# The eighth block pair of a 2048 x 2048 product by Strassen, with its weights prepared earlier and on VectorE

## The chip, the cores and the metric

One core of one Trainium2 chip runs the kernel. The metric is the device time of one execution in microseconds (us), the median of three runs. The core has TensorE (PE, matrix products into PSUM), VectorE (DVE), ScalarE (ACT), GpSimd (POOL) and SyncE (SP, which here only issues transfers). Each engine works through its own list of instructions in order, and waits on semaphores for the others.

## What is computed

```python
S, D, H, Dh = 2048, 512, 32, 16
Fh = 688
x = A_x                                    # (1, 2048, 512) bf16
# A: linear attention
q, k, v = split_heads(x @ wqkv)
phi(t) = concat(softmax(t @ w_phi), softmax(-(t @ w_phi)))
o = (phi(q) @ (phi(k)^T v)) / (phi(q) @ sum_s phi(k) + 1e-6)
a = o @ wo
# B: spatial gating
z  = gelu(x @ w_in)                        # (2048, 1376)
z1 = z[:, :Fh];  z2 = layernorm(z[:, Fh:])
g  = w_sp @ z2 + b_sp[:, None]             # (2048 x 2048) @ (2048 x 688)
b  = (z1 * g) @ w_out
# mix
s = sigmoid((x * gate_w).sum(-1))
out = s * a + (1 - s) * b
```

## The kernel before

The tokens are cut into 16 tiles of 128. The work comes in four stretches.

**z2 half (up to 24 us).** For each token tile, `z2_tile` multiplies x by the second half of w_in (eight matmuls of 344 columns into a PSUM tile `zp`, of which there are three), ScalarE takes the gelu into `z2raw`, and VectorE takes mean and variance (two L226, one L227). After every fourth tile `z2_norm` lets GpSimd compute `rstd` (L287, L290) and VectorE write the normalised `z2all` (four L292). x arrives transposed by SP's transfers (L142, L149).

**z1 half (24 to 44 us).** `z1_tile` does the same product with the first half of w_in, and ScalarE's gelu (L280) writes `z1all`; a `zp` tile comes free when its gelu has read it. Two calls of `fold` multiply the query and key weights with w_phi (after tiles 6 and 11) and ScalarE copies the results out (L336, L334). `z_sum` lets VectorE form the sums T1 to T4 of z2 (eight L400).

**Main stretch (44 to 125 us).** Sixteen steps, one for each key tile. A step holds the product of the next key tile (`k_tile`, L438), of the value tile (`v_tile`, L481), the accumulation of an earlier tile (`kv_acc`, L498), one entry of the list `steps` of the spatial product, and in the steps of `Q_AT` a query tile (`q_tile`). For each key or query tile ScalarE takes two exponentials (L442), VectorE a sum over 1024 elements (L446) and a reciprocal, and GpSimd a scaling (L461, L462). For a value tile VectorE writes `vr` (L487), which frees the bank `V_BANK` that all value tiles but the second share.

**Last stretch (from 125 us).** The rest of `steps`, the attention outputs and the final products of each token tile.

**The spatial product.** w_sp has 16 row tiles. Row tiles p and p+8 are a pair. `w_load(p)` brings a pair in by two transposing transfers (L170, ring of four buffers `wsp`). For the pairs 1 to 7 (`MIXED`) the 2 x 2 block product of the pair with z2 is done by Strassen's method in Winograd's form: seven products P1 to P7 of eight matmuls each (`product`, L563) instead of eight. Pair 0 (`PLAIN`) is done directly by `plain`: four pieces (two row tiles, two column halves) of sixteen matmuls each (L531), one piece in each of the steps 0 to 3.

A Strassen pair needs its weights prepared. `w_size` (ScalarE, L341, twice) sums absolute values of the two row tiles, a small activation adds the two sums into `wsum16` (L346), `w_level` multiplies that with ones on TensorE (L350), so that every partition has the level, and VectorE takes `wdown` and `wup` from it (L352, L355). `w_scale` (ScalarE, L374) scales the second row tile in place, and `w_sum` (VectorE, L361, L381, L383) forms S3, S1, S2 and S4, in that order. S4 overwrites A12, so it comes after P2. When a product is done, ScalarE or VectorE takes it from PSUM: `seed` after P1 or P4, `scaled` after P6, P7 and P4 (L545), an activation after P2 (L583), and `plus` after P7 and P3 (VectorE, L570); `gated` multiplies each result into `z1all` (GpSimd, L577). P5, and then P3, accumulate in one PSUM bank, and the `plus` of P7 reads that bank between them.

**What sets the order.** On TensorE and ScalarE the program's order is kept as written (`manual_schedule`); on the other engines a scheduler orders by readiness at build time. `steps` is a list that is filled pair by pair, and `work_at` says in which step a pair's `w_size`, `w_scale`, `w_sum` and `w_load` are called. SP issues all transfers of the first stretches in one queue: x, w_in, the bias row `brow`, the first part of the query and key weights, eight small `wphi` pieces, the second part, the value weights `wv_sb`, then three pairs of w_sp.

Of the kernel before, what the change touches and what calls it, by code (L numbers as in the profile page):

```python
# [14 lines left out]
P = 128  # L15
# [20 lines left out]
PLAIN = (0,)  # L36
MIXED = (1, 2, 3, 4, 5, 6, 7)
# [4 lines left out]
def kernel(  # L42
# [112 lines left out]
    nc.sync.dma_start(out=brow[0:NT, :], in_=B_b_sp.rearrange("(t p) -> t p", p=P))  # L155
    heads = A_w_phi.rearrange("(kc u) e f -> u e kc f", u=8)
    for qk in (1, 0):
        nc.sync.dma_start_transpose(
            out=wqkT[:, qk * NDT:(qk + 1) * NDT, :], in_=A_wqkv[:, qk * D:(qk + 1) * D])
        for u in range(8 if qk == 1 else 0):  # L160
            us = slice(u * DH, (u + 1) * DH)
            nc.sync.dma_start(out=wphi[us, :, us], in_=heads[u])
    nc.sync.dma_start(out=wv_sb[:, :, :], in_=A_wqkv[:, 2 * D:3 * D].rearrange("(dt p) n -> p dt n", p=P))
# [9 lines left out]
    for p in range(3):  # L173
        w_load(p)
# [54 lines left out]
    def z2_tile(tt):  # L229
        z2_out(tt, z_mm(tt, w_z2, FH + 1))  # L230
# [44 lines left out]
    def z1_of(tt, c0, c1):  # L275
        return z1all[:, tt, c0:c1]
# [62 lines left out]
    def w_size(p, h):  # L339
        mute = ring.tile([P, NT * P], BF16, name="mute", bufs=1)  # L340
        nc.scalar.activation(  # L341
            out=mute[:, :],
            in_=wraw[p][:, h * NT:(h + 1) * NT, :].rearrange("p s c -> p (s c)"),
            func=AF.Abs, accum_out=wsum[:, p, h:h + 1])
        if h == 1:
            nc.scalar.activation(  # L346
                out=wsum16[:, p:p + 1], in_=wsum[:, p, 1:2], func=AF.Identity, bias=wsum[:, p, 0:1])

# [8 lines left out]
    HALVED = (5, 6)  # L357

# [13 lines left out]
    def w_scale(p):  # L372
        tail = wraw[p][:, NT:2 * NT, :].rearrange("p s c -> p (s c)")
        nc.scalar.activation(out=tail.bitcast(FP16), in_=tail, func=AF.Copy, scale=wup[:, p:p + 1])  # L374
# [103 lines left out]
    def v_tile(tt, rk, bank):  # L478
        v_ps = bank_tile(bank)
# [13 lines left out]
        return vr  # L493
# [33 lines left out]
    def plain(t, j):  # L527
        x = bank_tile(next_turn("mm", 2))[:, 0:HF]
        h = t // HS
        for st in range(NT):  # L530
            nc.tensor.matmul(  # L531
                x, lhsT=wraw[t % HS][:, h * NT + st, :], rhs=z2all[:, st, j * HF:(j + 1) * HF],
                start=(st == 0), stop=(st == NT - 1))
        zu = z1_of(t, j * HF, (j + 1) * HF)
        nc.vector.scalar_tensor_tensor(
            out=zu, in0=x, scalar=bT[:, t:t + 1], in1=zu, op0=ALU.add, op1=ALU.mult)
# [175 lines left out]
    Q_AT = (1, 3, 6, 9, 12, 15)  # L712
    with tc.manual_schedule(engines={mybir.EngineType.PE, mybir.EngineType.Activation}):
# [3 lines left out]
        for tt in range(NT):  # L717
# [3 lines left out]
            late = steps[0][0][0] is product and steps[0][0][2] in (1, 6)  # L721
# [3 lines left out]
            pend.append((tt, ek, v_tile(tt, rk, V_BANK if tt != 1 else X_TAGS[2])))  # L725
# [112 lines left out]
```

## Time and profile before

| | |
|---|---|
| three runs | 199.76, 200.1, 200.7 us; median 200.1 |
| the profiled execution | 199.89 us, of which the span from first to last instruction is 198.2 |
| granted TensorE clock | 1.0 |
| z2 half, z1 half | TensorE to 24.06 us, to 44.12 us |
| ScalarE and VectorE, 46 to 62 us | 15.4 and 13.5 of 16 us busy |
| DMA engines, 22 to 26 us | 0.17 and 0.07 mean busy share in two slices of 2 us |

Times below are us from the start of the span, durations us or, where marked, ns. PE is TensorE's matmul row and PEld its weight load. A row of instructions gives line, engine, operation, tiles, shapes and count, then the busy total in us and the mean of one in ns, then the engine's idle time in front of them and what ended it.

### The profile page before, as it was taken

How to read it: one execution, taken by the hardware profiler on the slowest of the kernel's cores; microseconds unless marked ns; L12 is line 12 of the kernel's file. 1: busy time of each engine (PE TensorE's matmuls, PEld its weight loads, DVE VectorE, ACT ScalarE, POOL GpSimd, SP SyncE). 2: the span in 40 equal slices, each digit the busy share in tenths (PEclk: the TensorE clock that was granted, in tenths of full speed). 3: DMA queues.
4: the chain of work that ended last, by engine and by line, in shares of the span. 5: the costliest groups of instructions: out<-in, count | busy, mean ns of one | idle time of the engine just before them, and what ended most of it. 6: DMA issues, size and time to landing. Idle time of an engine off the chain costs nothing.

```text
span 198.2 us, 3988 instructions
## 1 busy us (share of the span) xinstructions
PE 193.4 (98%) x1466; PEld 115.6 (58%) x1484; DVE 144.4 (73%) x268; ACT 136.2 (69%) x216; POOL 88.2 (45%) x132
## 2 busy tenths in 40 slices
PE   8999999999999999999999999999999999999994
PEld 4666666665555665565565566665555555654542
DVE  4478977914989999798798796998968569554300
ACT  3466667889899679789789788569675476232222
POOL 6021023000552685885795788645536245420400
PEclk9999999999999999999999999999999999999999
DMA  6799479999803930750870666697688898595261
GB/s 193 134 190 218 86 156 194 207 202 208 244 3 64 200 58 0 159 109 0 160 107 3 132 133 69 143 205 146 138 161 181 113 220 149 119 149 132 65 147 53
DMA packets 89210, 26.50 MB, mean 134 GB/s; under 512 B 84536, under 2 KB 89064, under 8 KB 89192
## 3 DMA queue, kind: packets, MB, share of 16 engines
q1 hardware_dynamic: 86448, 23.32, 62.2%
q10 hardware_dynamic: 2600, 2.42, 5.0%
q0 software_dynamic: 144, 0.52, 0.8%
q8 instruction: 11, 0.18, 0.4%
q14 instruction: 7, 0.06, 0.1%
HBM read 3.45 MB, written 2.10 MB: 28 GB/s over the span
## 4 chain that ended last, share of the span: by engine, by line
PE 92%; SPq 2%; DMA 2%; DVE 1%; issue 1%; DVEq 0%
PE mm L563 27%; PE zp L208 19%; PE mm L438 14%; PE mm L634 8%; PE mm L481 7%; PE mm L629 6%; PE mm L531 5%; DMA oT<-o 2%; PE kvacc L498 2%; PE at L604 2%; SPq L524 1%; PE zp L239 1%; DVE o L615 1%; SPq L475 1%; PE zp L327 0%
## 5 line engine op out<-in xcount | busy, mean ns | idle before, releaser
L208 PE MATMUL zp<-w_z,xT 128*128 128x344 bf16 (+1 forms) x254 | 38.5, 311 | 0.0
L577 POOL TENSOR_TENSOR z1all<-c,z1all 128x344 bf16<-128x344 f32 x28 | 25.5, 916 | 21.0 <-DVE c L570 7.2
L563 PEld LDWEIGHTS <-wsp 128*128 128x128 f16 (+1 forms) x280 | 26.6, 98 | 13.9
L208 PEld LDWEIGHTS <-xT 128*128 128x128 bf16 x254 | 24.4, 98 | 12.3 <-DMA xT<-in_A_x_dram 0.4
L563 PE MATMUL mm<-z2all,wsp 128*128 128x344 f16 x168 | 27.9, 309 | 0.0
L341 ACT ACTIVATE mute<-wsp 128x2048 bf16<-128x2048 bf16 x14 | 26.8, 1914 | 0.4 <-ACT ob L646 0.4
L446 DVE TENSOR_REDUCE zs<-eq 128x64 f32<-128x1024 bf16 x16 | 19.3, 1209 | 7.5 <-ACT eq L442 7.5
L646 ACT ACTIVATE ob<-mm,g_inv 128x512 bf16<-128x512 f32 (+1 forms) x16 | 10.9, 680 | 19.8 <-PE mm L634 17.8
L446 DVE TENSOR_REDUCE zs<-ek 128x64 f32<-128x1024 bf16 x16 | 19.2, 1203 | 7.2 <-ACT ek L442 7.2
L634 PE MATMUL mm<-w_out_sb,uT 128*128 128x512 bf16 (+2 forms) x101 | 23.3, 366 | 0.1
L461 POOL TENSOR_TENSOR ratio<-zs,rk 128x32 f32<-128x32 f32 x16 | 8.2, 511 | 32.8 <-DVE rk L455 29.7
L442 ACT ACTIVATE eq<-mm 128x512 bf16<-128x512 f32 x32 | 17.3, 593 | 6.9 <-PE mm L438 6.4
L563 PE MATMUL mm<-zmix,wmix 128*128 128x344 f16 x112 | 18.6, 309 | 0.0
L563 PE MATMUL mm<-zmix,wsp 128*128 128x344 f16 x112 | 18.6, 309 | 0.0
L462 POOL TENSOR_TENSOR eq<-eq,ratio 128x512 bf16<-128x512 bf16 x16 | 17.4, 1089 | 1.3
L438 PEld LDWEIGHTS <-xT 128*128 128x128 bf16 x128 | 11.8, 98 | 10.5
L462 POOL TENSOR_TENSOR ek<-ek,ratio 128x512 bf16<-128x512 bf16 x16 | 17.9, 1119 | 0.0
L442 ACT ACTIVATE ek<-mm 128x512 bf16<-128x512 f32 x32 | 17.3, 603 | 0.5 <-PE mm L438 0.2
L374 ACT ACTIVATE wsp<-wsp,wup 128x2048 f16<-128x2048 bf16 x7 | 14.0, 2001 | 4.5 <-DVE wup L355 4.5
L223 ACT ACTIVATE z2raw<-zp 128x688 bf16<-128x688 f32 x16 | 11.9, 745 | 7.4 <-PE zp L208 7.0
L481 PE MATMUL mm<-wv_sb,xT 128*128 128x512 bf16 x62 | 16.3, 379 | 0.1
L629 PE MATMUL mm<-wo_t,oT 128*128 128x512 bf16 (+2 forms) x65 | 16.3, 366 | 0.2
(100 smaller groups left out, 308.2 us busy)
## 6 DMA issues: line engine op xcount, KB each, us to landing
out_dram<-ob ACTq DMA_DIRECT2D x14, 128.0 KB, 2.5
w_z<-in_B_w_in_dram SPq DMA_DIRECT2D x2, 344.0 KB, 5.8
w_out_sb<-in_B_w_out_dram SPq DMA_DIRECT2D x1, 640.0 KB, 4.8
wv_sb<-in_A_wqkv_dram SPq DMA_DIRECT2D x1, 512.0 KB
wo_t<-in_A_wo_dram POOLq DMA_DIRECT2D x1, 512.0 KB, 5.8
w_z<-in_B_w_in_dram ACTq DMA_DIRECT2D x2, 172.0 KB, 3.4
w_z<-in_B_w_in_dram SPq DMA_DIRECT2D x2, 172.0 KB, 3.3
wsp<-in_B_w_sp_dram SPq DMA_TRANSPOSE x16, 5.2
```

What stands on the lines that cost most here:

```text
L208: nc.tensor.matmul(zp[:, j, 0:n], lhsT=xT[:, dt, tt * P:(tt + 1) * P], rhs=wt[:, dt, j * HF:j * HF + n], start=(dt == 0), stop=(dt == NDT ...
L341: nc.scalar.activation(out=mute[:, :], in_=wraw[p][:, h * NT:(h + 1) * NT, :].rearrange("p s c -> p (s c)"), func=AF.Abs, accum_out=wsum[: ...
L374: nc.scalar.activation(out=tail.bitcast(FP16), in_=tail, func=AF.Copy, scale=wup[:, p:p + 1])
L438: nc.tensor.matmul(ps[:, :], lhsT=xT[:, dt, tt * P:(tt + 1) * P], rhs=w[:, dt, :], start=(dt == 0), stop=(dt == NDT - 1))
L442: nc.scalar.activation(out=e[:, :, a, :], in_=ps[:, :].rearrange("p (h f) -> p h f", f=DH), func=AF.Exp, scale=1.0 - 2.0 * a)
L446: nc.vector.tensor_reduce(out=z[:].rearrange("p h a -> p (h a)"), in_=e[:].rearrange("p h a f -> p (h a) f"), axis=AX.X, op=ALU.add,)
L462: nc.gpsimd.tensor_tensor(out=e[:, :, 1, :], in0=e[:, :, 1, :], in1=ratio[:, :, None].to_broadcast([P, H, DH]), op=ALU.mult)
L481: nc.tensor.matmul(v_ps[:, :], lhsT=xT[:, dt, tt * P:(tt + 1) * P], rhs=wv_sb[:, dt, :], start=(dt == 0), stop=(dt == NDT - 1))
L563: nc.tensor.matmul(x, lhsT=w_part(p, wa)[:, st, :], rhs=zsums[zb][:, st, :], start=(k in OPENS and st == 0), stop=(st == HS - 1), skip_gro ...
L577: nc.gpsimd.tensor_tensor(out=zu, in0=o, in1=zu, op=ALU.mult)
L629: nc.tensor.matmul(acc, lhsT=oTs[n][:, g, :], rhs=wo_t[:, g, c0:c1], start=start and g == 0, stop=stop and g == NG - 1)
L634: nc.tensor.matmul(acc, lhsT=uTs[n][:, ft, :], rhs=w_out_sb[:, ft, c0:c1], start=start and ft == 0, stop=stop and ft == NFT - 1)
```

## The change

Pair 0 goes from `plain` to the seven products. Its list entries are P1 and P5 in step 0, P2 in step 1, P6, the next pair's P1 and P7 in step 2, P4 and P3 in step 3. Pair 1 has its P1 already done in step 2, so step 4 holds two products instead of three. From step 5 on the entries are the same. Its preparation lies in the z1 half: VectorE takes the largest absolute value of the second row tile (`w_peak`) in place of one `w_size`, ScalarE keeps the `w_size` of the first row tile, VectorE adds twice the one to the other (`w_both`), `w_level(0)` stands on TensorE behind z1 tile 12, and VectorE scales the tail and forms S3, S1 and S2. One half of pair 1 is measured with `w_peak` too, and pair 1 is scaled on VectorE. `brow`, `wphi` and `wv_sb` are loaded from GpSimd's queue, ahead of its first `veps`, and no longer from SP's; SP loads four pairs of w_sp at the start. `z_sum` is called behind the tiles 1 to 8, the second `fold` behind tile 10. The second value tile goes to the upper half of `kvacc` and no longer to a bank of the products. Queries are in the steps 1, 4, 8, 11, 13 and 15, in place of 1, 3, 6, 9, 12 and 15.

In the built program VectorE's list for the z1 half reads: the first `zmix`, four `z2all`, three `zmix`, the first peak, four `zmix`, `wsum16` of pair 0, the peak of pair 1, `wdown`, `wup`, the scaling of pair 0, S3, S1, S2, and then the first two key sums of the main stretch. GpSimd's list has the ten transfers, then both `veps` and both `rstd` of the first eight tiles, and VectorE writes the first eight `z2all` together behind the first half statistics of tile 8.

```diff
-PLAIN = (0,)
-MIXED = (1, 2, 3, 4, 5, 6, 7)
+MIXED = tuple(range(NP))
...
+    def load_small():
+        heads = A_w_phi.rearrange("(kc u) e f -> u e kc f", u=8)
+        nc.gpsimd.dma_start(out=brow[0:NT, :], in_=B_b_sp.rearrange("(t p) -> t p", p=P))
+        for u in range(8):
             us = slice(u * DH, (u + 1) * DH)
-            nc.sync.dma_start(out=wphi[us, :, us], in_=heads[u])
-    nc.sync.dma_start(out=wv_sb[:, :, :], in_=A_wqkv[:, 2 * D:3 * D].rearrange("(dt p) n -> p dt n", p=P))
+            nc.gpsimd.dma_start(out=wphi[us, :, us], in_=heads[u])
+        nc.gpsimd.dma_start(
+            out=wv_sb[:, :, :], in_=A_wqkv[:, 2 * D:3 * D].rearrange("(dt p) n -> p dt n", p=P))
...
-    for p in range(3):
+    for p in range(4):
         w_load(p)
...
+    def w_peak(p, h):
+        nc.vector.tensor_reduce(
+            out=wsum[:, 0, 1:2], in_=wraw[p][:, h * NT:(h + 1) * NT, :].rearrange("p s c -> p (s c)"),
+            axis=AX.X, op=ALU.max, apply_absolute_value=True)
+
+    def w_both(p, h):
+        nc.vector.scalar_tensor_tensor(
+            out=wsum16[:, p:p + 1], in0=wsum[:, 0, 1:2], scalar=2.0, in1=wsum[:, p, 1 - h:2 - h],
+            op0=ALU.mult, op1=ALU.add)
...
+    SCALED_ON_DVE = (0, 1)
...
     def w_scale(p):
         tail = wraw[p][:, NT:2 * NT, :].rearrange("p s c -> p (s c)")
+        if p in SCALED_ON_DVE:
+            nc.vector.tensor_scalar(
+                out=tail.bitcast(FP16), in0=tail, scalar1=wup[:, p:p + 1], scalar2=None, op0=ALU.mult)
+            return
         nc.scalar.activation(out=tail.bitcast(FP16), in_=tail, func=AF.Copy, scale=wup[:, p:p + 1])
...
             z2_tile(tt)
+            if tt == 2:
+                load_small()
...
         b_T()
-        turn["zp"] += 1
         for tt in range(NT):
             z1_tile(tt)
-            if tt % 2 == 1:
-                z_sum(tt // 2 // 4, tt // 2 % 4)
-            if tt in (6, 11):
+            if 0 < tt < 9:
+                z_sum((tt - 1) // 4, (tt - 1) % 4)
+            if tt in (6, 10):
                 later = fold(1 if tt == 6 else 0)
-            if tt in (7, 8, 12, 13):
+            if tt in (7, 8, 11, 12):
                 later.pop(0)()
+            if tt == 5:
+                w_peak(0, 1)
+            if tt == 9:
+                w_size(0, 0)
+            if tt == 10:
+                w_both(0, 1)
+            if tt == 12:
+                w_level(0, zp_tile()[:, 0, :])
+                w_scale(0)
+                w_sum(0, 3)
+                w_sum(0, 1)
+            if tt == 14:
+                w_peak(1, 0)
...
-    LOAD_AT = {3: 1, 4: 4, 5: 7, 6: 10, 7: 13}
-    SIZE_AT = {1: (0, 1, 2), 2: (2, 3, 4), 6: (14, 16, 17), 7: (18, 19, 20)}
+    LOAD_AT = {4: 3, 5: 6, 6: 9, 7: 12}
+    SIZE_AT = {1: (0, 0, 2), 6: (14, 16, 17), 7: (18, 19, 20)}
...
+        if p == 0:
+            steps.append(first[:2])
+            del first[:2]
+            n = 1
         steps += [first, middle, [(product, p, 4), (product, p, 3)]]
...
-    Q_AT = (1, 3, 6, 9, 12, 15)
+    Q_AT = (1, 4, 8, 11, 13, 15)
...
+            if tt == SIZE_AT[1][2]:
+                w_both(1, 0)
-            late = steps[0][0][0] is product and steps[0][0][2] in (1, 6)
+            late = steps[0][0][2] in (1, 6)
...
-            pend.append((tt, ek, v_tile(tt, rk, V_BANK if tt != 1 else X_TAGS[2])))
+            pend.append((tt, ek, v_tile(tt, rk, kvacc[:, 4:8, :].rearrange("p g c -> p (g c)") if tt == 1 else bank_tile(V_BANK))))
```

More of the change, by code (lines that the diff above doesn't have):

```diff
@@ L154 @@
             out=w_z1[:, 2 * h:2 * h + 2, :], in_=w_in_v[:, 2 * h:2 * h + 2, 0:FH])
-    nc.sync.dma_start(out=brow[0:NT, :], in_=B_b_sp.rearrange("(t p) -> t p", p=P))
-    heads = A_w_phi.rearrange("(kc u) e f -> u e kc f", u=8)
     for qk in (1, 0):
@@ L159 @@
             out=wqkT[:, qk * NDT:(qk + 1) * NDT, :], in_=A_wqkv[:, qk * D:(qk + 1) * D])
-        for u in range(8 if qk == 1 else 0):
+    def load_small():
+        heads = A_w_phi.rearrange("(kc u) e f -> u e kc f", u=8)
+        nc.gpsimd.dma_start(out=brow[0:NT, :], in_=B_b_sp.rearrange("(t p) -> t p", p=P))
+        for u in range(8):
             us = slice(u * DH, (u + 1) * DH)
-            nc.sync.dma_start(out=wphi[us, :, us], in_=heads[u])
-    nc.sync.dma_start(out=wv_sb[:, :, :], in_=A_wqkv[:, 2 * D:3 * D].rearrange("(dt p) n -> p dt n", p=P))
+            nc.gpsimd.dma_start(out=wphi[us, :, us], in_=heads[u])
+        nc.gpsimd.dma_start(
+            out=wv_sb[:, :, :], in_=A_wqkv[:, 2 * D:3 * D].rearrange("(dt p) n -> p dt n", p=P))
     wraw, wmix = {}, {}
@@ L344, in w_size @@
             func=AF.Abs, accum_out=wsum[:, p, h:h + 1])
-        if h == 1:
+        if h == 1 and p > 1:
             nc.scalar.activation(
                 out=wsum16[:, p:p + 1], in_=wsum[:, p, 1:2], func=AF.Identity, bias=wsum[:, p, 0:1])
+    def w_peak(p, h):
[6 more added lines that the diff above has]
+            op0=ALU.mult, op1=ALU.add)
     def w_level(p, ps):
@@ L476, in q_tile, with v_tile @@
         eqTs[n] = eqT
-    def v_tile(tt, rk, bank):
-        v_ps = bank_tile(bank)
+    def v_tile(tt, rk, v_ps):
         for dt in range(NDT):
@@ L525, in u_T @@
         uTs[n] = uT
[L527 to L536, printed above, removed]
-    LOAD_AT = {3: 1, 4: 4, 5: 7, 6: 10, 7: 13}
-    SIZE_AT = {1: (0, 1, 2), 2: (2, 3, 4), 6: (14, 16, 17), 7: (18, 19, 20)}
+    LOAD_AT = {4: 3, 5: 6, 6: 9, 7: 12}
+    SIZE_AT = {1: (0, 0, 2), 6: (14, 16, 17), 7: (18, 19, 20)}
     PRODUCTS = {1: (0, "A11", "B11"), 6: (1, "S2", "T2"), 5: (2, "S1", "T1"), 2: (0, "A12", "B21"),
@@ L678 @@
         n, after = len(steps), MIXED[MIXED.index(p) + 1:][:1] if p in MIXED else ()
-        if p in PLAIN:
-            steps += [[(plain, t, j)] for t in (p, p + HS) for j in range(2)]
-            continue
         opened = p - 1 in MIXED
@@ L687 @@
             first.append(middle.pop(0))
+        if p == 0:
+            steps.append(first[:2])
+            del first[:2]
+            n = 1
         steps += [first, middle, [(product, p, 4), (product, p, 3)]]
         for k, lag in ((3, -1), (1, -1), (2, 0), (4, 1)):
-            at(n + lag, w_sum, p, k)
+            if p > 0 or lag >= 0:
+                at(n + lag, w_sum, p, k)
+        if p == 0:
+            continue
         s0, s1, s2 = SIZE_AT.get(p, (n - 5, n - 4, n - 3))
-        at(s0, w_size, p, 0)
+        if p > 1:
+            at(s0, w_size, p, 0)
         at(s1, w_size, p, 1)
         at(s2, w_scale, p)
-    for p in range(3, NP):
+    for p in range(4, NP):
         at(LOAD_AT[p], w_load, p)
```

## The prediction

> **What bounds the kernel now.** I read the chain of waits first, then TensorE's own waits, then the time lines of VectorE and ScalarE over the z1 half and the first steps.
>
> ```profile
> span 198.2 us, 3988 instructions
> PE 193.4 (98%) x1466; PEld 115.6 (58%) x1484; DVE 144.4 (73%) x268; ACT 136.2 (69%) x216; POOL 88.2 (45%) x132
> PE 92%; SPq 2%; DMA 2%; DVE 1%; issue 1%; DVEq 0%
> ...
> 46.72 2.33 PE mm L531 x16
> ...
> L531 PE MATMUL mm<-z2all,wsp 128*128 128x344 f16 x64 | 10.0, 309 | 0.0
> ```
>
> The span is TensorE's work without a gap: a matmul less is time less, and any wait put into TensorE's list is time more. VectorE's 73% is a mean. In the z1 half it looks like this (start, length, group, and in brackets its wait):
>
> ```profile
> 30.99 0.82 DVE L400 TENSOR_TENSOR zmix<-z2all 128x1376 f16<-128x1376 f16 x1
> 33.05 1.56 DVE L292 TENSOR_SCALAR z2all<-z2raw,mv,rstd 128x688 f16<-128x688 bf16 x4 [1.24 <-POOL rstd L290]
> 34.54 1.65 DVE L400 TENSOR_TENSOR zmix<-z2all 128x1376 f16<-128x1376 f16 x2
> 36.11 0.87 DVE L400 TENSOR_TENSOR zmix<-zmix,z2all 128x1376 f16<-128x1376 f16 x1
> 36.89 0.86 DVE L400 TENSOR_TENSOR zmix<-z2all 128x1376 f16<-128x1376 f16 x1
> ...
> 39.36 0.88 DVE L400 TENSOR_TENSOR zmix<-z2all,zmix 128x1376 f16<-128x1376 f16 x1
> 47.47 2.35 DVE L446 TENSOR_REDUCE zs<-ek 128x64 f32<-128x1024 bf16 x2 [7.23 <-ACT ek L442]
> ```
>
> VectorE is behind: it ends the z2 statistics at 31, 7 us after TensorE has left that half, and is free only from 40.2 to 47.5.
>
> **Matmuls removed.** A direct piece is 16 matmuls in 2.33 us, 0.1457 each. 64 become 7 x 8 = 56: -1.17. One `w_level` is added; the matmul of `b_T`, as small, stretched the distance of two gelus from 1.17 to 1.19 (24.08 to 25.27): +0.02.
>
> **The level matmul behind z1 tile 12** is where I see the loss: TensorE stops there until VectorE has written `wsum16`, and z1 tiles 13 to 15 and the whole main stretch stand behind it.
>
> TensorE's arrival: ScalarE gets a `w_size` behind gelu 9.
>
> ```profile
> 36.47 0.74 ACT L280 ACTIVATE z1all<-zp 128x688 bf16<-128x688 f32 x1
> 37.63 0.74 ACT L280 ACTIVATE z1all<-zp 128x688 bf16<-128x688 f32 x1 [0.42 <-PE zp L208]
> 38.80 0.74 ACT L280 ACTIVATE z1all<-zp 128x688 bf16<-128x688 f32 x1 [0.42 <-PE zp L208]
> ...
> 48.28 1.93 ACT L341 ACTIVATE mute<-wsp 128x2048 bf16<-128x2048 bf16 x1
> 50.08 0.22 ACT L341 ACTIVATION_READ_ACCUMULATOR mute<-wsp 128x1 f32 x1
> ```
>
> Gelu 9 runs from 36.47, its successor can start 0.64 later (the distance where gelu and copy follow at once, 32.27 to 32.91), and `w_size` occupies 1.89 (48.28 to 50.17): gelu 10 runs from 39.00 to 39.74 instead of from 37.63. Tile 12 needs tile 10's `zp` (three buffers, the second `fold` now taking one ahead of tile 11). TensorE, with tile 10 done at 37.63, `fold` 0.58 and tile 11 1.17, would start tile 12 at 39.38 and starts at 39.80: 0.4 lost, tile 12 done at 40.97. Behind it tile 13 would wait for gelu 11 until 41.35 in any case, so ScalarE alone costs 0.8.
>
> VectorE's arrival: the peak reduces 2048 values. No row has that; the row of 1024 takes 1203 ns, and its successor starts 1.13 later (62.40 to 63.53), which is 1024 elements at 0.96 GHz and 0.06. So 2.13 + 0.06 = 2.2, against a lower end of 1.1 (the z2all rows' 0.372 per 688, times 3). I take 2.2, the same operation on the same type. Its place is at 36.89 by the rows above, then four zmix of 0.8: `wsum16` at 42.3, done at 42.45. The new order of the statistics changes this a little. GpSimd's first two rstd now come both after the mean of tile 7 (16.2 + 0.6 + 1.05 = 17.9 for the first), VectorE waits there 0.7 and at tile 8 0.4, then at the third group 1.1 as before; instead of three waits of 1.1. It reaches the first zmix at 30.75, not 30.99. So `wsum16` at 42.2, TensorE on at 42.25. Tiles 13, 14 and 15 follow; 15 needs the `zp` of the level, which VectorE reads behind the second peak (42.15 + 2.2, done 44.5), and starts at 44.65. The z1 half ends at 45.8 against 44.12: **+1.7**, between 0.8 (VectorE in time) and 2.1 (no earlier start and wdown late).
>
> **Behind it in the z1 half.** wup at 44.6, the scaling, S3 1.2, S1 0.6, S2 0.6: done at 47.9. The scaling has no row: three times the z2all row gives 1.1, between 0.6 (half of it) and 2.0 (ScalarE's L374). It is hidden: P5 wants S1 at 45.8 + 3 x 0.865 + 1.17 = 49.6, and the first key sum, at 3.35 after the half's end, comes at 49.2. Without this cover each us of it would be a us of P5. The Trainium skill, "VectorE: DVE Perf Modes", section "The perf-mode tier table (the rule you actually need)", gives 693 ns for a `tensor_scalar` on 2048 bf16 values in SBUF; by it both scalings would be 0.4 shorter, and the sum lower by at most that.
>
> **Steps 0 to 4 on VectorE.** Removed: four pieces' output (L535, 4 x 0.52 = 2.1). Added: S4 1.2, the scaling of pair 1 1.1, two `plus` of 0.55, `w_both` 0.15; one query's sum and reciprocal (1.5) goes from step 3 to 4. The tight place is P3 of pair 0, which waits for the `plus` of P7. From the end of P2, VectorE needs 1.25 (it is at a key sum) + S4 1.2 + reciprocal 0.47 + query sum 1.13 + vr 0.6 + level and reciprocals 0.36 + key sum 1.13 + gate 0.35 + scaling 1.1 + reciprocals 0.58 + S3 1.2 + plus 0.48 = 9.85. TensorE needs five tiles of 0.865, four products of 1.167 and two accumulations of 0.26: 9.5. That is a wait of 0.35, but S3 and S4 go up when GpSimd works beside them:
>
> ```profile
> 59.98 1.90 DVE L361 SCALAR_TENSOR_TENSOR wmix<-wsp,wup 128x1024 f16<-128x1024 bf16 x1 [0.19 <-ACT wsp L374]
> 71.01 2.08 DVE L361 SCALAR_TENSOR_TENSOR wsp<-wsp,wup,wmix 128x1024 f16<-128x1024 bf16 x1
> 99.66 1.19 DVE L361 SCALAR_TENSOR_TENSOR wsp<-wsp,wup,wmix 128x1024 f16<-128x1024 bf16 x1
> ```
>
> With both at 2 it is 1.9; with a scaling of 0.6 and both at 1.2 nothing. I take **+0.4**. Later VectorE has about 2 us free per pair (1.40 + 0.25 + 0.26 in front of its groups from 91 to 96), so nothing is carried on.
>
> **Small loads.** GpSimd is idle from 3.9 to 12.1. A transfer of 512 KB took it 0.99 to issue (L754); ten of at most that end by 13.8, before the mean of tile 7 at 16.2. On SP they took 0.39, 3.83 and 0.58, so w_sp starts 5 us earlier, at 22.5. Pair 0 has landed by 30.5 (one issue of 2.8, then 5.2 to land), before the peak at 36.7; without this cover, from the old 27.5, it would land at 35.5. What `wv_sb` does to x is open: TensorE already waits for x tile 8.
>
> ```profile
>   DMA xT<-in_A_x_dram: 0.4, 1
> ```
>
> The software queue's 0.8% of 16 engines is 1.6 us for one such load; x waits between nothing and that, as at 12 to 14 us the engines are full (share 1.20) and before it half free (0.55). I take **+0.1**. The Trainium skill, "Trainium Kernel Development and Optimization", section "Key Constraints", says that transfers of SP, ACT and POOL run on the same 16 engines and interleave, so that another issuer saves issue time only. By this `wv_sb` delays x if both are in flight; no run here shows it yet.
>
> **At nothing.** ScalarE loses 4.5 us in steps 0 to 4 (a scaling, a `w_size`, an addition) and gets 3 (seed, two c, u2, u3). GpSimd gets four multiplications of 0.92 where it waits for VectorE. Pair 4's load waits for P3 instead of the last piece (62.7), some 2 us later; its first reader is in step 8, at 85. The later queries' transposes are read from 125 us on.
>
> **Sum.** -1.17 + 0.02 + 1.7 + 0.4 + 0.1 = +1.05. On the profiled execution's 199.89 (198.2 and 1.7 around it) that is 200.95; the median of the runs lies 0.2 higher: **201.2**.
>
> **Rivals.**
> - ScalarE alone: VectorE writes `wsum16` before 41, so only gelu 10 holds TensorE, and P3 finds its bank free. For it: VectorE's waits at rstd (three of 1.1, one of 1.24) could shrink. Against: they sum to less than what is needed with the peak's 2.2. -1.15 + 0.8: 199.7.
> - The clean gain, on the other side: the level finds everything ready, nothing else waits. Decided by one point: `wsum16` before TensorE would be there, at 40.5, and gelu 10 before 39.4. Against it is the list itself, with 2.2 more in front of what ended at 40.2 before. 199.0.
> - GpSimd late: a small transfer costs more to issue than the one row. From 1.25 each (end past 16.4) the first rstd, the z2 sums, and so `wsum16` slip one for one; at 1.5 each by 2.5: 203.6. Against: small ones should cost less than L754's 0.99.
> - `wv_sb` in front of x tile 8: the whole 1.6: 202.7. The 0.4 above speaks for it, SP's spacing of 1.27 per transfer against it.
>
> **Chances.** Forecast 0.45 (own range 200.4 to 202.3), ScalarE alone 0.18, clean gain 0.13, GpSimd late 0.12, x late 0.12. The range 199.2 to 203.0 leaves out the clean gain and half of the late GpSimd. Under 0.5% (1.0 us) a change can't be told from none here. Faster: the clean gain, 0.13. The same, up to 201.1: ScalarE alone and 0.18 of the forecast's 0.45, 0.36. Slower: 0.51.
>
> **What would show it.** Right: TensorE's wait at the level, on VectorE's `wsum16`, between tiles 12 and 13, of over 1 us, with the main stretch starting near 45.8; the peak's row at 2.2; 56 matmuls for pair 0; a short wait at P3 on L570's successor. Wrong: no wait at the level, a peak below 1.2, ten issues beyond 16 us, or a longer wait for x.

## The result: 5.0 us slower, and where the profile after puts them

The changed kernel takes 204.97 us (median of 6 runs, 204.68 to 205.49), the kernel before 199.93 in the same comparison. The ratio is 1.025, with a 95% interval of 1.0226 to 1.0274. The sign of the prediction held, its size did not: 201.2 was named, and the upper end of the range was 203.0.

The profiled execution took 205.49, with a span of 203.4 and a granted clock of 1.0. The head of its page, its chain of waits and one row of the groups:

```profile
span 203.4 us, 4014 instructions
PE 194.0 (95%) x1477; PEld 114.2 (56%) x1477; DVE 158.7 (78%) x278; ACT 136.5 (67%) x219; POOL 97.4 (48%) x146
...
PE 57%; DVE 23%; issue 5%; DMA 5%; POOL 4%; SPq 3%; ACT 3%; DVEq 0%; POOLq 0%
...
L583 PE MATMUL mm<-z2all,wsp 128*128 128x344 f16 x192 | 31.9, 309 | 2.0 <-DVE c L590 2.0
```

Before, TensorE held 92% of the chain, and behind its start its one wait was 0.15, near 181 us. Now it holds 57%, VectorE has 23%, and the products themselves stand behind `c`, the output of `plus`. The time line of TensorE's matmuls from 10 us on, only those groups that waited (start, length, group, wait):

```profile
14.26 1.34 PE L211 MATMUL zp<-w_z,xT 128*128 128x344 bf16 x8 [0.96 <-DMA xT<-in_A_x_dram]
16.74 9.53 PE L211 MATMUL zp<-w_z,xT 128*128 128x344 bf16 x64 [1.13 <-DMA xT<-in_A_x_dram]
42.01 1.33 PE L211 MATMUL zp<-w_z,xT 128*128 128x344 bf16 x8 [0.33 <-ACT z1all L283]
43.74 0.16 PE L363 MATMUL zp<-wsum,ones_sq 128*128 128x1 bf16 x1 [0.40 <-DVE wsum L358]
65.38 1.33 PE L583 MATMUL mm<-z2all,wsp 128*128 128x344 f16 x8 [0.61 <-DVE c L590]
69.18 1.33 PE L583 MATMUL mm<-zmix,wsp 128*128 128x344 f16 x8 [0.47 <-DVE c L590]
81.43 1.33 PE L583 MATMUL mm<-z2all,wsp 128*128 128x344 f16 x8 [0.26 <-DVE c L590]
126.83 1.33 PE L583 MATMUL mm<-z2all,wsp 128*128 128x344 f16 x8 [1.11 <-DVE c L590]
```

So there are three losses in three places: x arrives late (tiles 7 and 8), the z1 half stops at tile 12 and at the level matmul, and four products wait for a `plus`: P3 of pair 0, P5 and P3 of pair 1, P3 of pair 4. A wait costs a little more than its bracket: the products before and at 65.38 start 1.94 apart, without a wait 1.17, so 0.77 for a bracket of 0.61. Where a sum is made below, each wait has that 0.16 added. The wait of 0.15 near 181, which only the kernel before has, counts 0.31 in the same way: there the starts are 1.49 apart, not 1.17.

The span can be cut at three marks that every kernel of this study has: the last gelu of the z2 half (24.08 before), the first value tile (45.69) and the last group of matmuls (194.99). The differences to the kernel before, in the profiled executions:

| kernel | z2 half | z1 half | rest | to the last group |
|---|---|---|---|---|
| after | +2.23 | +1.07 | +1.77 | +5.07 |
| small loads on SP | -0.04 | +2.79 | +1.76 | +4.51 |
| value weights on SP | +0.42 | +1.90 | +1.80 | +4.12 |
| earlier queries | +1.51 | +1.08 | -0.71 | +1.88 |
| before, small loads on GpSimd | +1.35 | -0.01 | -0.30 | +1.04 |
| before, later queries | +0.12 | -0.01 | +1.88 | +1.99 |
| value weights on SP, earlier queries | +0.10 | +1.89 | -0.60 | +1.39 |
| the same, and the peak over a quarter | +0.10 | +0.87 | -0.59 | +0.38 |
| all relieved | +0.28 | +0.02 | -0.68 | -0.38 |

The experiments below make these terms come and go one at a time.

### The profile page after: what moved, and what is told of

The parts are those of the page before. It is cut to its first block, busy times and chain, and to the rows that moved or that the text cites. A ratio compares the mean times of both kernels' runs of the same rounds, so it can differ in the third digit from the quotient of the medians.

```text
span 203.4 us, 4014 instructions
## 1 busy us (share of the span) xinstructions
PE 194.0 (95%) x1477; PEld 114.2 (56%) x1477; DVE 158.7 (78%) x278; ACT 136.5 (67%) x219; POOL 97.4 (48%) x146
## 3 DMA queue, kind: packets, MB, share of 16 engines
q0 software_dynamic: 576, 1.07, 2.2%
## 4 chain that ended last, share of the span: by engine, by line
PE 57%; DVE 23%; issue 5%; DMA 5%; POOL 4%; SPq 3%; ACT 3%; DVEq 0%; POOLq 0%
PE mm L583 21%; PE mm L654 10%; PE mm L470 9%; PE mm L649 7%; DVE zs L478 5%; PE mm L512 3%; DMA xT<-in_A_x_dram 3%; SPq L141 3%; DVE bn L229 3%; DVE z2all L295 3%; PE zp L211 2%; DVE zmix L418 2%; PE at L624 2%; DVE vr L518 2%; DVE rk L487 2%
## 5 line engine op out<-in xcount | busy, mean ns | idle before, releaser
L583 PEld LDWEIGHTS <-wsp 128*128 128x128 f16 (+1 forms) x320 | 30.5, 98 | 19.1 <-issue 3.2
L597 POOL TENSOR_TENSOR z1all<-c,z1all 128x344 bf16<-128x344 f32 x32 | 31.3, 983 | 20.7 <-DVE c L590 7.2
L583 PE MATMUL mm<-z2all,wsp 128*128 128x344 f16 x192 | 31.9, 309 | 2.0 <-DVE c L590 2.0
L493 POOL TENSOR_TENSOR ratio<-zs,rk 128x32 f32<-128x32 f32 x16 | 7.1, 445 | 31.1 <-DVE rk L487 31.0
L583 PE MATMUL mm<-zmix,wsp 128*128 128x344 f16 x128 | 21.3, 309 | 0.5 <-DVE c L590 0.5
L583 PE MATMUL mm<-zmix,wmix 128*128 128x344 f16 x128 | 21.3, 309 | 0.0
L229 DVE BATCH_NORM_STATS2 bn<-z2raw 128x6 f32<-128x344 bf16 x32 | 14.5, 491 | 5.2 <-ACT z2raw L226 5.2
L494 POOL TENSOR_TENSOR eq<-eq,ratio 128x512 bf16<-128x512 bf16 x16 | 17.9, 1116 | 1.3
L392 ACT ACTIVATE wsp<-wsp,wup 128x2048 f16<-128x2048 bf16 x6 | 12.0, 1998 | 8.0 <-DVE wup L368 8.0
L494 POOL TENSOR_TENSOR ek<-ek,ratio 128x512 bf16<-128x512 bf16 x16 | 16.9, 1058 | 0.0
```

Source lines behind the costliest of these rows:

```text
L229: nc.vector.bn_stats(out=bn6[:, tt, j, :], in_=z2v[:, j, :])
L494: nc.gpsimd.tensor_tensor(out=e[:, :, 1, :], in0=e[:, :, 1, :], in1=ratio[:, :, None].to_broadcast([P, H, DH]), op=ALU.mult)
L583: nc.tensor.matmul(x, lhsT=w_part(p, wa)[:, st, :], rhs=zsums[zb][:, st, :], start=(k in OPENS and st == 0), stop=(st == HS - 1), skip_gro ...
L597: nc.gpsimd.tensor_tensor(out=zu, in0=o, in1=zu, op=ALU.mult)
```

## The experiments

Every label was compared with the kernel before on the same chip, whose median lay between 199.7 and 200.1.

### The small loads

The first of three kernels undoes the moved loads, the second only the 512 KB of `wv_sb`, the third adds the moved loads to the kernel before and nothing else.

```diff
 # e1_small_on_sp: after, with
-            if tt == 2:
-                load_small()
+    nc.sync.dma_start(out=brow[0:NT, :], ...)
...
+            nc.sync.dma_start(out=wphi[us, :, us], in_=heads[u])
...
+    nc.sync.dma_start(out=wv_sb[:, :, :], ...)
 # e2_wv_on_sp: after, with
-        nc.gpsimd.dma_start(out=wv_sb[:, :, :], ...)
+    nc.sync.dma_start(out=wv_sb[:, :, :], ...)
 # e4_before_small_pool: before, with
-    nc.sync.dma_start(out=brow[0:NT, :], ...)
...
-            nc.sync.dma_start(out=wphi[us, :, us], in_=heads[u])
...
-    nc.sync.dma_start(out=wv_sb[:, :, :], ...)
...
+            if tt == 2:
+                load_small()
```

> The changed kernel with all small loads back on SP's queue, in their old places. Theory A (the loads from GpSimd's queue hold x tiles 7 and 8 back, and the 2.2 us that this costs also lets VectorE catch up): TensorE's wait for x falls from 2.1 to 0, its wait at the level matmul grows from 0.4 to about 1.4, since VectorE's list then ends where the rows of the kernel before put it (wsum16 near 42.4, TensorE there at 41.1), and the main stretch starts at 46.0 in place of 47.3: about 203.7. Rival B (each wait has its own price): the level stays at 0.4 and the time falls by the whole 2.2, to 202.8. Rival C (x is late for another reason): x still waits 2, 205.

> The changed kernel with only the 512 KB of value weights back on SP's queue; brow and the eight wphi pieces (2 KB each) stay on GpSimd's. If it is the 512 KB that holds x back: wait for x 0, otherwise as with all loads on SP, about 203.7, or a little less, as w_sp starts some 4 us earlier. If it is the nine small ones (their runs of 32 bytes): wait for x stays near 2, 205.

> The kernel before with only the small loads moved to GpSimd's queue. Theory A: this alone makes TensorE wait 2.1 us for x, and nothing behind it takes that back: 202.1. Rival (the wait for x comes only with the rest of the change): 199.9.

Measured: with all small loads on SP 205.64 (204.51 to 206.66; ratio 1.0286, 1.0234 to 1.0337), with `wv_sb` alone on SP 204.02 (1.0229, 1.0165 to 1.0293), the kernel before with the loads on GpSimd 201.99 (1.0124, 1.008 to 1.0168). In the first two TensorE no longer waits for x. In the third it waits where it did not, though by 0.69 and not by the 2.1 that was expected:

```profile
15.86 9.53 PE L212 MATMUL zp<-w_z,xT 128*128 128x344 bf16 x64 [0.69 <-DMA xT<-in_A_x_dram]
```

This execution is the fastest of its four. Its z2 half ends 1.35 later than before and its last group starts 1.04 later; in the median the kernel takes 2.3 more, of which 0.4 lies outside the span. So the moved loads are a cause by themselves, and the 512 KB are the part that matters: the second kernel keeps the nine small pieces on GpSimd.

Yet taking the x wait away in the changed kernel gains little: up to the last group 0.95 with `wv_sb` on SP and 0.56 with all small loads there, in the profiled executions. The medians gain 0.95 and nothing, and the runs of one of these kernels lie up to 2.8 apart, so the times alone don't show a gain. Both were expected at 203.7. The time line of TensorE with all small loads on SP says where the gain goes:

```profile
39.75 1.33 PE L208 MATMUL zp<-w_z,xT 128*128 128x344 bf16 x8 [0.33 <-ACT z1all L280]
43.19 0.16 PE L360 MATMUL zp<-wsum,ones_sq 128*128 128x1 bf16 x1 [2.12 <-DVE wsum L355]
```

The level matmul waited 0.40 and now waits 2.12, where 1.4 was expected. TensorE got there 2 us earlier, VectorE did not: in the changed kernel VectorE's first `zmix` is only 0.97 later than before (31.96 against 30.99), while TensorE is 2.23 late. The waits for x and for the level share their time. In this kernel VectorE also waits 0.45 for w_sp at the peak (37.30), the cover that the prediction named for the old place of the loads.

Whether it is the queue or the time at which the 512 KB are in flight, a further kernel tells: after, with the earlier queries, and `wv_sb` still on GpSimd's queue but behind `rstd` of tile 7, so that its transfer is issued at 19.9 and not at 8.6.

```diff
 # e12_wv_pool_late: after, with Q_AT = (1, 3, 6, 9, 12, 15) and
-        nc.gpsimd.dma_start(out=wv_sb[:, :, :], ...)
...
                 z2_norm(list(range(tt - 3, tt + 1)))
+            if tt == 7:
+                nc.gpsimd.tensor_copy(out=wv_sb[:, 0, 0:8], in_=rstd[:, 0:8])
+                nc.gpsimd.dma_start(out=wv_sb[:, :, :], ...)
```

> The changed kernel with old queries, and the value weights still on GpSimd's queue, but behind the rstd of tile 7 (a small write into their tile makes them wait), at about 19 us and no longer at 8.6. Theory A (what holds x back is that the 512 KB are in flight together with x): no wait for x, about 201.5, as with the weights on SP. Rival (a load from GpSimd's queue slows the transposes whenever it is issued, or the queue itself is the cost): SP's next transposes are late and the w_sp data with them, 202.4 as with the early load.

Measured: 201.58 (1.0081, 1.006 to 1.0102). The wait for x is 0.17, the z2 half ends 0.12 earlier than before. So it is the time in flight and not GpSimd's queue as such; the same load at the early time from another queue was not run. The level waits 0.97 and P3 of pair 0 0.59.

### The queries

The changed kernel with the old steps of the queries, and the kernel before with the new ones:

```diff
 # e3_queries_old: after, with
-    Q_AT = (1, 4, 8, 11, 13, 15)
+    Q_AT = (1, 3, 6, 9, 12, 15)
 # e9_before_queries_late: before, with
-    Q_AT = (1, 3, 6, 9, 12, 15)
+    Q_AT = (1, 4, 8, 11, 13, 15)
```

> The changed kernel with queries in the steps 1, 3, 6, 9, 12, 15. Theory A (the query in step 13 puts its sum on VectorE between P7 and the plus that P3 of pair 4 waits for, in step 15): the wait of 1.1 us at 126.8 goes; the waits of pair 0 and 1 (0.6 and 0.5 in steps 3 and 4) stay or grow by up to 1, as the query of step 3 comes back: 203.7 to 205. Rival B (VectorE has too much work in all, and a wait only changes its place): the sum of TensorE's waits for the plus stays at 2.5 or more, 205.

> The kernel before with queries in the steps 1, 4, 8, 11, 13, 15 and nothing else. Theory A (a query in step 13 stands on VectorE in front of the plus that P3 of pair 4 needs in step 15, whatever pair 0 does): a wait of about 1.1 there, 201.0. Rival (it takes the added work of pairs 0 and 1): no wait, 199.8.

Measured: 202.36 (1.0121, 1.0095 to 1.0147), 2.6 less than the changed kernel, and 202.03 (1.0091, 1.0065 to 1.0116), 2.0 more than before. Both differ from what was expected by 1 us or more: more waits hang on the queries than the one at pair 4. The time line of TensorE shows which. After, with the old queries, from 44 us on, one is left of four:

```profile
64.66 1.33 PE L583 MATMUL mm<-z2all,wsp 128*128 128x344 f16 x8 [0.61 <-DVE c L590]
```

Before, with the new queries, from 44 us on:

```profile
65.24 1.33 PE L563 MATMUL mm<-z2all,wsp 128*128 128x344 f16 x8 [0.49 <-DVE z1all L535]
123.64 1.33 PE L563 MATMUL mm<-z2all,wsp 128*128 128x344 f16 x8 [1.12 <-DVE c L570]
```

P3 of pair 4 waits the same 1.1 in a kernel that has no Strassen pair 0 at all. VectorE's time line of the changed kernel, ahead of that product, tells why (S3 in two halves, the sum of the query, S1, `plus`):

```profile
118.54 2.75 DVE L375 SCALAR_TENSOR_TENSOR wmix<-wsp,wup 128x512 f16<-128x512 bf16 x2
121.21 1.21 DVE L478 TENSOR_REDUCE zs<-eq 128x64 f32<-128x1024 bf16 x1
...
124.28 1.02 DVE L399 TENSOR_TENSOR wsp<-wsp 128x1024 f16<-128x1024 f16 x1
...
126.22 0.56 DVE L590 SCALAR_TENSOR_TENSOR c<-mm,wdown,u 128x344 f32<-128x344 f32 x1
```

The query of step 13 puts a sum of 1.21 and a reciprocal of 0.34 into VectorE's list between S3 and the `plus` that P3 waits for, in the steps where another pair's S3, S1 and S2 are due. With the query in step 12 the two halves of S3 take 0.76 and 0.78 (117.95 and 120.36), not 2.75 together, and `plus` ends at 123.3 with nobody waiting.

At P5 of pair 1 the reason is another one. It waits for the `plus` of P3 of pair 0, and VectorE is no later there: this `plus`, of 0.47, starts at 68.66 in the changed kernel, 3.28 behind the start of P3, and at 67.93 with the old queries, 3.27 behind it. What differs is TensorE's list. With the old queries the query tile of step 3 stands between P3 and P5 (one of its four matmuls is missing from the trace):

```profile
66.04 0.81 PE L470 MATMUL mm<-wq_p,xT 128*128 128x512 bf16 x3
66.68 1.03 PE L470 MATMUL mm<-wk_p,xT 128*128 128x512 bf16 x4
...
68.69 1.33 PE L583 MATMUL mm<-zmix,wsp 128*128 128x344 f16 x8
```

It takes TensorE 0.86, as long as the other tiles of a step, and so covered the `plus`. Without it TensorE comes to P5 too early. The 0.49 of the kernel before with the new queries is the same case: VectorE's last output of pair 0 ends 4.93 behind the start of the last piece with the new queries and with the old. At P3 of pair 1 (0.26) VectorE's list holds the same instructions up to the `plus` with both placings, but with the later query it waits 0.45 for ScalarE's scaling, and S3 and S1 take 1.93 and 1.21 instead of 1.29 and 0.78.

### Both undone

```diff
 # e5_wv_sp_queries_old: after, with both
-        nc.gpsimd.dma_start(out=wv_sb[:, :, :], ...)
+    nc.sync.dma_start(out=wv_sb[:, :, :], ...)
-    Q_AT = (1, 4, 8, 11, 13, 15)
+    Q_AT = (1, 3, 6, 9, 12, 15)
```

> The changed kernel with the value weights on SP's queue (no wait for x) and the queries in their old steps (one wait for the plus, 0.6). Left are ScalarE's 0.5 at z1 tile 12, VectorE's 1.2 at the level, and 0.8 at P3 of pair 0, against 1.17 saved: 0.5 + 1.4 + 0.8 - 1.15 = +1.5 on the 199.7 of before, 201.3. If the two parts overlap (the time that VectorE gains by one is lost at the other), 202 or more.

Measured: 201.49 (1.0063, 1.004 to 1.0086), for an expected 201.3. All of TensorE's waits from the z2 half to the end:

```profile
39.91 1.33 PE L210 MATMUL zp<-w_z,xT 128*128 128x344 bf16 x8 [0.27 <-ACT z1all L282]
42.43 0.16 PE L362 MATMUL zp<-wsum,ones_sq 128*128 128x1 bf16 x1 [1.19 <-DVE wsum L357]
64.12 1.33 PE L582 MATMUL mm<-z2all,wsp 128*128 128x344 f16 x8 [0.67 <-DVE c L589]
```

This is the kernel that the prediction described, with its two mistaken terms taken out, and it stands at the predicted waits and near the predicted time.

### The z1 half

Two ways to take the level's wait away: put the level, the scaling, S3 and S1 behind tile 15, or shorten the peaks to 512 of their 2048 values (the levels then leave out three quarters of the second row tile).

```diff
 # e6_level_later: e5, with
-            if tt == 12:
+            if tt == 15:
                 w_level(0, zp_tile()[:, 0, :])
 # e7_peak_quarter: e5, with
-            ... in_=wraw[p][:, h * NT:(h + 1) * NT, :] ...
+            ... in_=wraw[p][:, h * NT:h * NT + NT // 4, :] ...
```

> As the kernel with value weights on SP and old queries, but the level matmul of pair 0, its scaling, S3 and S1 stand behind z1 tile 15 and no longer behind tile 12. Theory A (TensorE only stops because the level stands too early in its list): the wait of 1.2 at the level goes, since wsum16 is written near 42.5 and TensorE is there at 44.7; P5 still finds S1: 1.3 less than that kernel, about 200.0. Rival (VectorE as a whole is late, so the wait moves to the first key tiles or P3): the wait at P3 grows by what the level loses, and the time stays at 201.3.

> As the kernel with value weights on SP and old queries, but each peak is taken over the first quarter of the row tile's values (512 of 2048), so that the scale differs; this measures what the peak's length costs. Theory A: the peak takes 0.6 and not 2.28, wsum16 is there at 40.8, before TensorE (41.1): the level's wait is 0, and ScalarE alone sets the end of the z1 half, by 0.5 to 0.8: 200.1 to 200.4. Rival (the wait at the level is not the peak's): the wait stays at 1.2, 201.3.

Measured: 200.86 (1.0036, 1.0022 to 1.0049), between the two times expected, and 200.79 (1.003, 1.0007 to 1.0052), 0.4 above its expectation. The level's wait is gone in both. With the quarter peaks only ScalarE's part is left in the z1 half, a wait of 0.33 and one of 0.22 for `z1all`, and the half is 0.87 longer than before: that is the rival "ScalarE alone", whose price was worked out as 0.8. So 1.02 of the 1.89 were the peak. With the level behind tile 15 a part comes back: P3 of pair 0 then waits 0.97, not 0.67: VectorE's S3, S1 and S2 now lie in the first steps, in front of what P3 waits for.

### The wait at P3 of pair 0

Is one instruction late there, or are the engines short of time in steps 0 to 4? Four kernels take something out of VectorE's way, and a fifth relieves everything at once.

```diff
 # e8_level_later_scale_act: e6, with
-    SCALED_ON_DVE = (0, 1)
+    SCALED_ON_DVE = (0,)
 # e10_first_query_later: e6, with
-    Q_AT = (1, 3, 6, 9, 12, 15)
+    Q_AT = (2, 3, 6, 9, 12, 15)
 # e11_relieved: e10, level at tile 12, quarter peaks, and
-            if tt == 9:
-                w_size(0, 0)
-            if tt == 10:
-                w_both(0, 1)
+            if tt == 10:
+                nc.vector.tensor_scalar(
+                    out=wsum16[:, 0:1], in0=wsum[:, 0, 1:2], scalar1=500.0, scalar2=None, op0=ALU.mult)
 # e13_size_moved: e8, with
-    SIZE_AT = {1: (0, 0, 2), 6: ...
+    SIZE_AT = {1: (0, 0, 2), 2: (1, 3, 4), 6: ...
```

`e14_all_relieved` is e13 with e11's quarter peaks and level, and the old queries. e11 and e14 leave out ScalarE's size of pair 0.

> As the kernel with the level behind tile 15, with the scaling of pair 1 back on ScalarE (2.0 there, 0.75 off VectorE). Theory A: VectorE writes the plus ahead of S3 now, so P3 of pair 0 does not wait; but ScalarE's list then has the size of pair 2 (1.9) and the scaling (2.0) ahead of u3, so P4 of pair 0, which waits for u3, is held by about 1: 200.9, the same time by another wait. Rival (ScalarE has the room): no wait at P4, 199.8.

> As the kernel with the level behind tile 15 (value weights on SP), but the first query is in step 2 and no longer in step 1 (2, 3, 6, 9, 12, 15). Theory A (the wait of P3 of pair 0 is VectorE's list between P2 and the plus, 9.85 us against TensorE's 9.5 by the prediction's rows): the first query's sum and reciprocal, 1.4, leave that list, and the wait of 1.0 goes: 199.7. Rival (VectorE is short of time over all of the steps 0 to 5): the wait turns up at P5 or P3 of pair 1, 200.9.

> As the kernel with the first query in step 2, with the level behind z1 tile 12 and its cause taken away: pair 0 is not measured by ScalarE at all (its scale is 500 times the peak), and both peaks are over the first quarter of the values. Theory A: with ScalarE's size, the long peak, the value weights on GpSimd's queue and the late queries gone, nothing waits and the eight matmuls show: 199.0 to 199.3, 0.8 to 1.1 less than before. Rival (something else in the change costs, such as the doubled work of GpSimd or the second value tile in kvacc): 199.9 or more.

> The kernel whose level comes behind tile 15 and whose pair 1 is scaled on ScalarE, with ScalarE's size of pair 2 moved from step 2 to step 1, so that it no longer stands in front of the input of P7's sum. If the waits at P3 of pair 0 are a matter of the order of lists in these steps (one late piece), the wait of 0.72 on ScalarE goes and the time falls from 200.92 to 200.2, the level with before. If VectorE and ScalarE are short of time over steps 0 to 4, the wait turns up at another product of pair 0 or 1 with 0.4 us or more, and the time stays within 0.3 of 200.9.

> The kernel with the value weights on SP and the earlier queries, and three reliefs at once: the peaks over a quarter of their width (512 values for 2048), no size of pair 0 on ScalarE (its level is 500 times the peak), pair 1 scaled on ScalarE with the size of pair 2 one step earlier. The numbers are scaled otherwise and the peaks leave out three quarters of the weights. If each wait found so far is a term of its own, the z1 half has none (main stretch from 44.4) and P3 of pair 0 at most 0.2: 199.3 us, 0.6 below before. If the waits move to the next product, the z1 half is clean and one wait of 0.6 or more stands in steps 2 to 4 nevertheless: 200.2.

| label | median | ratio | what waits after the z1 half |
|---|---|---|---|
| e8 | 200.92 | 1.0044 (1.0029 to 1.006) | P4 of pair 0: 0.72, on ScalarE; level of pair 2: 0.19 |
| e10 | 202.17 | 1.0104 (1.0076 to 1.0132) | P5 of pair 1: 0.95; an attention product: 0.99 |
| e11 | 201.89 | 1.0104 (1.0078 to 1.013) | P5 of pair 1: 0.94 |
| e13 | 200.46 | 1.0035 (1.0015 to 1.0056) | level of pair 1: 0.43 |
| e14 | 200.23 | 1.0017 (1.0007 to 1.0028) | level of pair 1: 0.54 |

The expectations of e10 (199.7) and e11 (199.0 to 199.3) were missed, that of e8 (200.9, by a wait at P4) was met. With pair 1 scaled on ScalarE, P3 of pair 0 waits no more for VectorE. In its place the product ahead of it, P4, waits for ScalarE, and the time stays. TensorE's time line of e8:

```profile
61.47 1.33 PE L582 MATMUL mm<-zmix,wsp 128*128 128x344 f16 x8 [0.72 <-ACT u L564]
```

ScalarE had a `w_size` of 1.90 and the scaling of 1.99 in front of `u`, which takes P7's result out of the bank that P4 goes on adding to. Moving the first query to step 2 frees P3 and stops the next product that needs its bank back from a `plus`, P5 of pair 1, which opens the bank of P3. TensorE's time line of e10:

```profile
67.44 1.33 PE L582 MATMUL mm<-zmix,wsp 128*128 128x344 f16 x8 [0.95 <-DVE c L589]
```

Moving one `w_size` of pair 2 a step forward (e13) takes the waits at P4 and P3 away altogether, and what is left is 0.43 at the level of pair 1, again behind ScalarE. Here the order in the lists mattered: both readings hold in part. The last kernel is the cleanest; TensorE's time line has one wait after the z2 half, and ScalarE's shows what it stands behind (two sizes, then four exponentials):

```profile
14.79 9.53 PE L210 MATMUL zp<-w_z,xT 128*128 128x344 bf16 x64 [0.48 <-DMA xT<-in_A_x_dram]
55.38 0.16 PE L362 MATMUL mm<-wsum,ones_sq 128*128 128x1 bf16 x1 [0.54 <-ACT eq L472]
```

```profile
49.02 1.94 ACT L343 ACTIVATE mute<-wsp 128x2048 bf16<-128x2048 bf16 x1
...
51.86 1.96 ACT L343 ACTIVATE mute<-wsp 128x2048 bf16<-128x2048 bf16 x1
...
54.19 1.14 ACT L472 ACTIVATE eq<-mm 128x512 bf16<-128x512 f32 x2
```

Its account closes to 0.1: the z1 half is 0.02 longer than before (the level matmul), and from the first value tile to the last group of matmuls it is 0.68 shorter. The eight matmuls give -1.17, the one wait +0.54 and 0.16, and the kernel before has the wait near 181 that is not there, -0.31: -0.78 for the -0.68. So the matmuls removed are worth what the prediction said. But its expectation of 199.3 was missed, and its median is 0.24 above the kernel before. What TensorE gains is lost behind it. In the profiled executions the last group starts 0.38 earlier, and the spans are both 198.2: the last output transfer is issued 0.80 behind the start of the last group in both kernels, and from the end of that issue to the end of the span it is 2.43 us, not 2.05. Another 0.39 in the median lies outside the span (below). Neither is explained by any run here.

No kernel of this study beats the one before.

## Why the prediction was right in sign and wrong in size

**The matmuls removed, -1.17.** Right, as far as e14's account goes, to 0.1.

**The level behind z1 tile 12, +1.7.** Right in place, mechanism and nearly in size. In the kernel without the other two losses (e5) the half is 1.89 longer, with the 1.19 at the level for VectorE's `wsum16` and 0.27 at tile 12 for gelu 10. In the changed kernel it is +1.07 and the wait at the level 0.40, below the 1 us that the prediction named as its sign, as the wait for x let VectorE catch up. The row of the peak came out at 2.28 for a predicted 2.2. VectorE's time line of the changed kernel in the z1 half:

```profile
31.96 0.82 DVE L418 TENSOR_TENSOR zmix<-z2all 128x1376 f16<-128x1376 f16 x1
...
37.86 2.28 DVE L353 TENSOR_REDUCE wsum<-wsp 128x1 f32<-128x2048 bf16 x1
...
43.44 0.15 DVE L358 SCALAR_TENSOR_TENSOR wsum<-wsum 128x1 bf16<-128x1 f32 x1
43.63 2.29 DVE L353 TENSOR_REDUCE wsum<-wsp 128x1 f32<-128x2048 bf16 x1
...
46.21 0.75 DVE L389 TENSOR_SCALAR wsp<-wsp,wup 128x2048 f16<-128x2048 bf16 x1
```

The scaling took 0.75, where the prediction had 1.1. The Trainium skill, "VectorE: DVE Perf Modes", section "The perf-mode tier table (the rule you actually need)", gives 693 ns for a `tensor_scalar` on 2048 bf16 values in SBUF, and the trace agrees with it better than with the estimate from the nearest row. In the z1 half nothing hung on it, as the prediction said.

**P3 of pair 0, +0.4.** The wait is there, in the named place, for the named `plus`: 0.61, with the 0.16 added 0.77. The working held better than the value chosen from it. VectorE's time line of the changed kernel over steps 2 and 3 (S4, the scaling of pair 1, its S3, `plus`):

```profile
56.61 1.94 DVE L375 SCALAR_TENSOR_TENSOR wsp<-wsp,wup,wmix 128x1024 f16<-128x1024 bf16 x1
...
62.42 0.74 DVE L389 TENSOR_SCALAR wsp<-wsp,wup 128x2048 f16<-128x2048 bf16 x1
...
63.66 1.18 DVE L375 SCALAR_TENSOR_TENSOR wmix<-wsp,wup 128x1024 f16<-128x1024 bf16 x1
64.76 0.56 DVE L590 SCALAR_TENSOR_TENSOR c<-mm,wdown,u 128x344 f32<-128x344 f32 x1
```

The list was 9.85 with S4 at 1.2 and the scaling at 1.1. With 1.94 and 0.75 it is 10.24, against TensorE's 9.5: 0.74. S4 had gone up beside GpSimd, S3 had not, so one of the two dear rows was the right value. The term was mis-sized by 0.4. The prediction's "when GpSimd works beside them" was too wide a condition: GpSimd worked beside this S3 too, but began 0.04 later (last section).

**The later queries, at nothing.** This is the first step that failed. "The later queries' transposes are read from 125 us on" looked at who reads a query's result, and not at what a query tile does in the steps that it leaves and enters: its 0.86 us on TensorE cover VectorE's work, and its sum stands in VectorE's list. "Nothing is carried on" went by two free us per pair, an average over steps. The runs showed three waits in its place, 0.47 at P5 of pair 1 (the cover is gone from step 3), 0.26 at P3 of pair 1 (the same query, now in step 4) and 1.11 at P3 of pair 4 (the sum of the one that moved from 12 to 13). In the profiled executions the rest of the span is 1.77 longer with the new queries and 0.71 shorter with the old, 2.48 between them; the same edit on the kernel before gives 1.88.

**x behind `wv_sb`, +0.1.** This is the second. It was the rival with a chance of 0.12, and its price was bounded at 1.6, the queue time of the one load that GpSimd's queue had before. That bound was no bound. SP's queue, the two large transfers of x, before:

```profile
10.09 4.14 SPq L149 DMA_TRANSPOSE xT<-in_A_x_dram  x2
```

and after:

```profile
10.24 6.36 SPq L148 DMA_TRANSPOSE xT<-in_A_x_dram  x2
```

They take 2.22 longer, and the z2 half ends 2.23 later. Of the three kernels with this load this execution is the dearest: with the same load the two take 5.66 and 5.82 in the kernel before with the small loads on GpSimd and in e3, and the half ends 1.35 and 1.51 later. In the thirteen kernels without it they take 4.01 to 4.78. GpSimd's time line of the changed kernel shows the transfers of 2 KB and the one of 512 KB being issued:

```profile
4.52 4.08 POOL L163 DMA_DIRECT2D wphi<-in_A_w_phi_dram  x8
8.59 0.79 POOL L164 DMA_DIRECT2D wv_sb<-in_A_wqkv_dram  x1
```

Last, the windows of 2 us of the changed kernel (after the window and its sum the busy time of PE, PEld, DVE, ACT and POOL; at the end the clock, the mean busy share of the DMA engines, and GB/s):

```profile
10.00:12.00 2.00, 2.00 (x16) 1.32 (x15) 1.93 (x8) 1.42 (x4) 0.00 (x0) 1.00 0.87 195
12.00:14.00 2.00, 1.30 (x9) 0.65 (x7) 1.93 (x7) 1.45 (x4) 0.23 (x1) 1.00 1.32 203
14.00:16.00 2.00, 1.34 (x8) 0.70 (x8) 1.26 (x4) 0.49 (x3) 0.00 (x0) 1.00 1.38 255
```

Before, these shares were 0.56, 1.20 and 1.17, with 107, 251 and 240 GB/s. From 10 to 12 the engines move more, as `wv_sb` comes in; from 12 to 14, where x is due, they are busier than before and move less. That they move less is this execution alone: the other two kernels with the load moved 278 and 262 GB/s there, and x was late all the same. The half-free stretch before 12 us did not take the load: it landed 5.2 after its issue, so at about 14. The Trainium skill, "Trainium Kernel Development and Optimization", section "Key Constraints", has transfers that SP, ACT and POOL issue interleave on the same 16 engines; the delayed x (6.36), and its return with `wv_sb` out of the way in e2 and e12 (4.07 and 4.06), agree with it. What it does not give is the size. No row before the change showed it either; the term should have had a free upper end, and the issue time of 1.27 per transfer, given as evidence against, says nothing of a queue that is shared.

**The rivals.** GpSimd late: wrong, the ten issues end at 9.4, and a small one takes 0.51. The clean gain is right in its condition (a z1 half at +0.02 and a `plus` in time), which only e14 comes near, with the reliefs that it needs.

**The sum.** The prediction's +1.05 becomes, from the profiled execution: x +2.23, z1 half +1.07, P3 of pair 0 +0.77, the three waits of the queries +2.32 (0.47, 0.26, 1.11 and three times 0.16), the matmuls -1.17, together +5.22. Less the wait near 181, which only the kernel before has (0.31), that is +4.91 of the +5.07 of the table. These are not prices one by one: with x in time the level waits longer, and the two halves together cost 1.99 in e5 and 3.30 in the changed kernel. The sign was not luck, for without both failed terms the change still costs 1.4 (e5).

## What to carry to other kernels

A step that is moved in an ordered program must be costed in the list of every engine that it issues to, not by who reads its result: at the new place beside what is due there, and at the old place by the work of others that its own time had covered. A transfer that is moved to another queue is moved in time too: if it is in flight with a transfer that sets the pace, its price is bounded by what the two share, not by its own row alone. Where an engine is busy for 10 us on end, as VectorE is in steps 1 to 4 here, removing one wait can move it to the next product; undo the causes together before judging one by itself.

## What the runs showed of the hardware

- A software-queue load of 512 KB in flight with two transposing transfers lengthened these: 5.66, 5.82 and 6.36 us in the three kernels that have it, 4.01 to 4.78 in the thirteen that don't. Moved to 19.9 us, it left them at 4.06 (e12).
- S3 and S4 (1024 elements per partition) take 1.28 us where GpSimd is idle (47.00 in the changed kernel), and the order of starting decides who is slowed. S3 at 63.66 took 1.18, and GpSimd's `ratio`, begun 0.04 later, 1.26 in place of 0.27. S3 at 73.66, begun 0.22 after a GpSimd scaling of 1.06, took 1.93. In six traces (before, after, e3, e5, e13, e14) all rows that began ahead of GpSimd's instruction took 1.18 to 1.29, and those that had 0.8 us or more of a scaling still before them 1.90 to 2.08. Three more took 1.94, as S4 at 56.61, where a scaling was about to end and GpSimd's next instruction began at once.
- The time around the span is not the same in all kernels: 1.73 us in the median for the kernel before, 1.75 for e5 and 1.71 for e12, but 2.12 for e14, 2.13 for e8 and 2.17 for the kernel before with the small loads on GpSimd, and 1.98 for the changed kernel. Within the span, the time from the start of the last group of matmuls to the end differs too: 3.20 before, 3.38 in the changed kernel, 3.57 in e14, 3.81 in e12. The profile does not show what either is, and no run here tells; it stays open. Open too is why e10 and e11 scatter (201.18 to 205.04 and 200.55 to 202.8), so that their verdicts rest on the waits more than on the times.
